# A recurrent gate and a merged feed-forward on one core: another order of all jobs, and 4 KB loads for four chunks

## The chip, the cores and the metric

The kernel runs on one core of a Trainium2 chip. A core has TensorE (PE in the profile: matrix products, into PSUM), VectorE (DVE), ScalarE (ACT), GpSimd (POOL) and SyncE (SP, which here issues the DMA transfers). The metric is the device time of one execution in microseconds.

## The reference

```python
# x, r_gate, i_gate: [4, 5824, 256]; a_param: [256]
a_base = sigmoid(a_param)
a_t    = exp(8 * sigmoid(r_gate) * log(clip(a_base, 1e-6, 1 - 1e-6)))
xg     = sqrt(max(1 - a_t * a_t, 1e-6)) * sigmoid(i_gate) * x
h      = a_t[:, t] * h + xg[:, t]          # for each t; y[:, t] = h
# y as [23296, 256]; w1, w2: [256, 1024]; w3: [1024, 1024]; w_out: [1024, 256]
out    = (((y @ w1) * (y @ w2)) @ w3) @ w_out
```

Inputs and output are f32.

## The kernel before

**Tiling.** The 23296 tokens are cut into 47 chunks: two of 256 tokens (0 and 1; their gates and their input are computed together under the name of chunk 0), 44 of 512, and one of 256 (46). Before the chunks flow, the kernel multiplies w3 by w_out once (the "fold": jobs Ft, Fc, Fm, Fe for eight pieces of w3) so that each chunk needs two products of 256 x 1024 and one of 1024 x 256.

**Jobs.** Every job has a short name, `ORDER` is a text of 2449 such words, and the last loop issues them in that order. Each engine works through its own words in that order, so the text fixes the queue of each engine. Per chunk c the words are:

- `r`, `i`, `x`: load the two gates and the input (DMA, issued by SP); `R`, `I`: tanh of a gate on ACT; `p`: plus 1 on POOL; `t c.half`: the gated input u, half a chunk at a time, on POOL (or DVE).
- `V`, `U`: turn the gate and u so that channels lie on the partitions and time runs along the row. For chunks 0, 2, 3, 4, 7 (gate) and 0, 2 to 7 (u) PE does it, for the others a transposing DMA does.
- `d c.cb`: the decay a = exp(...), on ACT, for one half cb of the channels; `s`: its square (on ACT, DVE or POOL, by the sets `AC_SQUARE` and `DV_SQUARE`); `q`: the root on ACT; `g`: the root times the turned u, on DVE (`gated`); `h c.cb`: the scan over time on DVE; `y`: the cast of h to bf16 (POOL, or by set DVE or ACT).
- `a c.mp.q`: one of the eight 128-row parts of y @ w1 on PE (two matmuls of 512 columns); `c`: its copy out of PSUM, on ACT or, for words in `DV_COPY`, on DVE; `b c.mp`: two such parts of y @ w2 on PE (four matmuls); `m c.mp`: the product of the two on DVE, into the tile `g_t`; `D c.j`: 128 rows of the last product, eight matmuls of 256 columns; `e`: copy out of PSUM (ACT, or DVE for `DV_EVAC`); `o`: store.
- `Lw`, `Cw`: load and cast of a weight; `A`: the rates from a_param; `W`: two matmuls on an identity whose result nobody reads; `E`: the identity's cast.

**Buffers.** `RINGS` gives the number of buffers of each kind: 2 for y @ w2 (`pb`), 4 PSUM banks shared by the parts of y @ w1, the last product and the turned tiles (`po`), 3 for the copies (`sa`) and for `g_t`, 2 for h, 4 for y, 6 for a and nrm. A `b` must wait until the `m` of the `b` two places earlier has read its buffer.

**Two layouts of a chunk's rows.** In most chunks, partition p holds the tokens p, p + 128, and so on, and a load reads rows of 1 KB. In the chunks for which PE turns both tiles (`long_rows`: 0, 2, 3, 4, 7), partition p holds four neighbouring tokens, a load reads 4 KB runs, and the turned tile comes out with time interleaved; `decay` and `gated` then read it with a step (`turned`) and write in order of time (`in_time`).

Of the kernel before, what the change touches and what calls it, by code (L numbers as in the profile page):

```python
# [23 lines left out]
def kernel(  # L24
# [190 lines left out]
    def decay(c, cb):  # L215
        w = width(c)
        if ("a", c) not in T:
            T["a", c] = ring(held, [P, NCB, CT], F32, name="a_t", tag="a")
# [4 lines left out]
        nc.scalar.activation(out=a, in_=pr, func=AF.Exp, scale=la4[:, cb:cb + 1], bias=la4[:, cb:cb + 1])  # L223
# [250 lines left out]
    def last(c):  # L474
# [32 lines left out]
        s7.0 I6 V5 r8 i8 V6 r9 x5 b3.3 d5.1 a3.0.1 d5.0 c3.0.1 c3.3.0 m3.3 p4 t4.0 t4.1 p5 s7.1 U4 a3.1.1 c3.1.1 s5.0  # L507
        I7 I8 D0.1 D0.0 b3.0 b3.1 a3.1.0 g4 h4.0 h4.1 s5.1 R8 R9 d6.0 d6.1 p6 y4 p8 t5.0 t5.1 D0.3 D0.2 m3.0 e0.0
        c3.1.0 a4.1.1 b4.1 a4.3.1 D2.0 D2.1 s6.1 q7 e2.0 q5 s6.0 x6 p7 t6.0 t6.1 c4.1.1 e0.1 m3.1 c4.3.1 x7 x8 o0.0
        i10 r11 V9 o2.0 a4.0.1 a4.1.0 c4.0.1 c4.1.0 m4.1 a4.2.0 b4.3 a4.3.0 U5 g5 h5.0 h5.1 c4.2.0 c4.3.0 q6 D2.3 D2.2  # L510
        e2.1 r12 r10 V8 o2.1 o0.1 i9 i11 x10 a4.0.0 U6 D3.0 a4.2.1 D3.1 b4.0 c4.0.0 I10 c4.2.1 e3.0 d9.1 d9.0 m4.3 g6
        y5 t8.1 t7.1 t7.0 m4.0 a5.1.0 b4.2 a5.1.1 a5.0.1 a5.0.0 b5.0 c5.1.1 c5.1.0 c5.0.0 m4.2 h6.1 U7 a5.3.1 c5.0.1
        s9.1 R10 c5.3.1 R11 d8.1 I9 m5.0 g7 h6.0 b5.1 D3.3 b5.3 D3.2 a5.2.1 a5.3.0 e3.1 R12 d8.0 m5.1 c5.2.1 c5.3.0
        h7.1 D4.2 a5.2.0 D4.3 e4.1 m5.3 i13 V10 o3.0 x9 p10 t8.0 y6 p9 s8.0 s9.0 h7.0 b6.0 a6.0.0 a6.0.1 y7 c5.2.0 I11
        I13 a6.2.1 a6.2.0 b5.2 s8.1 c6.0.0 c6.0.1 c6.2.0 D4.1 a6.1.0 D4.0 d10.1 c6.2.1 d10.0 e4.0 q9 a6.1.1 m6.0 m5.2
# [149 lines left out]
```

## Time and profile before

| | |
|---|---|
| time, median of 2 runs | 511.44 us (511.37 to 511.52) |
| profiled execution, first to last instruction | 509.1 us |
| PE busy | 501.7 us, 99% |
| ACT busy | 461.5 us, 91% |
| DVE busy | 431.8 us, 85% |
| POOL busy | 318.0 us, 62% |
| main DMA queue | 85.4% of 16 engines' span |

The span is that of one profiled execution, from its first to its last instruction; the time of a run has 2.3 us around it. Matmuls overlap each other in the profile: the next one starts before the modelled end of the last, so a wait shorter than this overlap does not show as idle time of PE. A row of the timeline gives start, busy time, engine, line, operation, tiles, shape and count, and in brackets the idle time in front of it and what ended it.

### The profile page before, as it was taken

How to read it: one execution, taken by the hardware profiler on the slowest of the kernel's cores; microseconds unless marked ns; L12 is line 12 of the kernel's file. 1: busy time of each engine (PE TensorE's matmuls, PEld its weight loads, DVE VectorE, ACT ScalarE, POOL GpSimd, SP SyncE). 2: the span in 40 equal slices, each digit the busy share in tenths (PEclk: the TensorE clock that was granted, in tenths of full speed). 3: DMA queues.
4: the chain of work that ended last, by engine and by line, in shares of the span. 5: the costliest groups of instructions: out<-in, count | busy, mean ns of one | idle time of the engine just before them, and what ended most of it. 6: DMA issues, size and time to landing. Idle time of an engine off the chain costs nothing.

```text
span 509.1 us, 8891 instructions
## 1 busy us (share of the span) xinstructions
PE 501.7 (99%) x3225; PEld 308.3 (61%) x3225; DVE 431.8 (85%) x417; ACT 461.5 (91%) x708; POOL 318.0 (62%) x269
## 2 busy tenths in 40 slices
...
GB/s 317 410 411 345 335 316 282 305 286 259 310 220 298 279 285 247 211 302 196 247 305 327 254 286 148 252 243 227 210 246 164 235 298 161 85 166 62 65 51 104
DMA packets 178048, 124.06 MB, mean 244 GB/s; under 512 B 87378, under 2 KB 174036, under 8 KB 178004
## 3 DMA queue, kind: packets, MB, share of 16 engines
q1 hardware_dynamic: 178000, 123.50, 85.4%
...
q14 instruction: 19, 0.16, 0.1%
...
## 4 chain that ended last, share of the span: by engine, by line
PE 92%; ACT 3%; DMA 2%; POOL 1%; DVE 1%; issue 1%; SPq 1%; ACTq 0%; DVEq 0%
PE po L357 30%; PE pb L299 29%; PE pa L299 29%; DMA wf<-in_moe_w_dram 2%; PE pw L436 1%; ACT sa L322 1%; PE ptr L200 1%; PE ptw L425 1%; POOL u_t L192 0%; DVE h_t L270 0%; SPq L151 0%; ACT ot L322 0%; SPq L407 0%; ACT L168 0%; ACT L238 0%
## 5 line engine op out<-in xcount | busy, mean ns | idle before, releaser
L337 DVE TENSOR_TENSOR g_t<-sa,pb 128x1024 bf16<-128x1024 bf16 (+1 forms) x188 | 218.7, 1180 | 58.9 <-PE pb L299 27.6
L299 PEld LDWEIGHTS <-w_sb 128*128 128x128 bf16 x1504 | 146.4, 98 | 144.1 <-issue 1.4
L322 ACT CAST sa<-pa 128x512 bf16<-128x512 f32 (+1 forms) x332 | 179.8, 591 | 27.1 <-PE pa L299 18.9
L299 PE MATMUL pa<-y_t,w_sb 128*128 128x512 bf16 (+1 forms) x752 | 190.2, 372 | 0.2 <-ACT sa L322 0.2
L299 PE MATMUL pb<-y_t,w_sb 128*128 128x512 bf16 (+1 forms) x752 | 184.9, 372 | 0.2 <-ACT w_sb L414 0.2
L357 PE MATMUL po<-wp_sb,g_t 128*128 128x256 bf16 (+1 forms) x1464 | 177.6, 272 | 0.0
L357 PEld LDWEIGHTS <-g_t 128*128 128x128 bf16 x1464 | 142.5, 98 | 39.5 <-issue 0.3
L282 POOL CAST y_t<-h_t 128x1024 bf16<-128x1024 f32 (+2 forms) x47 | 53.8, 1145 | 140.2 <-DVE h_t L270 136.1
L192 POOL TENSOR_TENSOR u_t<-i_t,x_t 128x512 bf16<-128x512 f32 (+1 forms) x90 | 123.3, 1387 | 3.8 <-DMA ut<-u_t 1.8
L270 DVE TENSOR_TENSOR_SCAN h_t<-a_t,h_t,nrm 128x512 f32<-128x512 f32 (+1 forms) x92 | 121.1, 1343 | 1.6
L233 POOL TENSOR_TENSOR nrm<-a_t 128x512 f32<-128x512 f32 x70 | 78.4, 1137 | 7.0 <-ACT a_t L223 4.0
L223 ACT ACTIVATE a_t<-rt,la 128x512 f32<-128x512 bf16 (+1 forms) x82 | 66.1, 823 | 0.0
L322 ACT COPY ot<-po 128x512 f32<-128x512 f32 x84 | 49.1, 589 | 13.2 <-PE po L357 12.9
L173 POOL TENSOR_SCALAR i_t<-i_t 128x1024 f32<-128x1024 f32 (+1 forms) x45 | 55.4, 1233 | 8.3 <-ACT i_t L168 8.3
L251 DVE SCALAR_TENSOR_TENSOR nrm<-nrm,ut 128x1024 f32<-128x1024 f32 (+1 forms) x39 | 53.2, 1365 | 5.2 <-ACT nrm L238 5.2
L168 ACT ACTIVATE i_t<-i_t 128x1024 f32<-128x1024 f32 (+1 forms) x46 | 48.5, 1063 | 0.3 <-DMA i_t<-in_i_gate_dram 0.2
L238 ACT ACTIVATE nrm<-nrm 128x1024 f32<-128x1024 f32 (+1 forms) x47 | 48.4, 1040 | 0.2
L162 ACT ACTIVATE th_r<-r_t 128x1024 bf16<-128x1024 f32 (+1 forms) x41 | 43.5, 1064 | 0.0
L320 DVE CAST sa<-pa 128x512 bf16<-128x512 f32 x36 | 23.5, 684 | 1.4 <-PE pa L299 0.8
L238 ACT ACT_TABLE_LOAD x17 | 21.8, 1283 | 0.4
L287 PE MATMUL warm<-ident 128*128 128x512 bf16 x32 | 10.7, 473 | 1.6 <-DVE ident L441 1.6
L231 ACT ACTIVATE nrm<-a_t 128x512 f32<-128x512 f32 x18 | 11.4, 645 | 0.0
...
## 6 DMA issues: line engine op xcount, KB each, us to landing
...
wf<-in_moe_w_out_dram SPq DMA_DIRECT2D x2, 512.0 KB, 10.2
rt<-th_r SPq DMA_TRANSPOSE x41, 4.7
ut<-u_t SPq DMA_TRANSPOSE x39, 4.4
```

What stands on the lines that cost most here:

```text
L173: (nc.vector if c in DV_PLUS else nc.gpsimd).tensor_scalar(t, t, 1.0, 1.0, op0=ALU.add, op1=ALU.mult)
L192: (nc.vector if (c, half) in DV_HALF else nc.gpsimd).tensor_mul(out=u, in0=t, in1=xt)
L223: nc.scalar.activation(out=a, in_=pr, func=AF.Exp, scale=la4[:, cb:cb + 1], bias=la4[:, cb:cb + 1])
L233: (nc.vector if (c, cb) in DV_SQUARE else nc.gpsimd).tensor_mul(out=n, in0=a, in1=a)
L238: nc.scalar.activation(out=n, in_=n, func=AF.Sqrt, scale=-1.0, bias=1.0)
L251: nc.vector.scalar_tensor_tensor(out=n, in0=n, scalar=1e-3, in1=T["pu", c][:, :, cols], op0=ALU.max, op1=ALU.mult)
L270: nc.vector.tensor_tensor_scan(h[:, cb, :], a[:, cb, :], n[:, cb, :], init, ALU.mult, ALU.add)
L282: (nc.vector if key in DV_CAST else nc.gpsimd).tensor_copy(out=y, in_=h)
L299: nc.tensor.matmul(out=dst, lhsT=w_sb[:, cb, m * P:(m + 1) * P], rhs=T["y", gates_of(c)][:, cb, span(c, mp)], start=(cb == 0), stop=(cb == ...
L322: nc.scalar.copy(out=dst, in_=src_ps)
L337: nc.vector.tensor_mul(out=T["g", z][:, 2 * mp:2 * mp + 2, span(c, mp)], in0=T["sa", c, mp][:, :, :w], in1=T["pb", c, mp][:, :, :w])
L357: nc.tensor.matmul(out=po, lhsT=T["g", c][:, k, j * P:(j + 1) * P], rhs=wp_sb[:, k, cols], start=(k == 0), stop=(k == KD - 1), skip_group_ ...
```

## The change

1. **A new order.** The same 2449 words in another order. The last 1049 words (from chunk 23's last product on) are the same as before, so all that moves lies in the chunks up to about 24 and in the start. With it the sets change that say which engine does a copy, a square, a copy of the result or a cast: 18 more copies go to DVE net (54 words instead of 36), 10 squares instead of 4 and 11 result copies instead of 7; two folds' copies leave DVE; two halves of u, one whole cast (chunk 24) and half of chunk 0's come to DVE; chunk 14's cast goes to ACT, and half of chunk 1's from ACT to POOL.
2. **Chunks 38 to 41** are loaded in 4 KB runs like the first ones, though a DMA turns their tiles. For 38 and 39 `decay` and `gated` read the turned bf16 tile with a step of 128 elements and write in order (`LONG_IN`); for 40 and 41 they read the bf16 tile in order and read and write the f32 tiles with a step of 4 elements (`LONG_OUT`). `gated` becomes two instructions of 512 elements per chunk instead of one of 1024.
3. **Chunk 42's scan** writes over its own input tile nrm (`OVER`) instead of into a buffer of the ring h.

```diff
--- before.py
+++ after.py
@@ -82,18 +82,20 @@
     TURN_U = {0, 2, 3, 4, 5, 6, 7}
     DV_TIMES = {0}
     DV_PLUS = set()
-    DV_HALF = set()
-    DV_SQUARE = {(0, 0), (0, 1), (5, 1), (9, 0)}
-    AC_SQUARE = {(2, 0), (2, 1), (3, 0), (4, 0), (4, 1), (5, 0), (6, 0), (6, 1), (7, 0), (8, 1), (9, 1), (11, 1), (12,
-        0), (12, 1), (13, 0), (14, 1), (15, 0), (15, 1)}
-    DV_CAST = {(1, 1)}
-    AC_CAST = {(1, 0)}
+    DV_HALF = {(5, 0), (17, 0)}
+    DV_SQUARE = {(0, 0), (0, 1), (3, 1), (13, 0), (18, 1), (19, 1), (21, 0), (23, 1), (24, 1), (28, 0)}
+    AC_SQUARE = {(2, 0), (2, 1), (3, 0), (4, 0), (4, 1), (5, 1), (7, 0), (8, 0), (8, 1), (11, 1), (12, 0), (12, 1),
+        (13, 1), (14, 1), (15, 0), (17, 1)}
+    DV_CAST = {24, (0, 1), (1, 1)}
+    AC_CAST = {14}
     DV_COPY = {(0, 0, 0), (0, 1, 0), (1, 0, 0), (1, 1, 0), (2, 0, 0), (2, 0, 1), (2, 1, 0), (2, 1, 1), (2, 2, 0), (2,
-        3, 0), (3, 0, 0), (3, 1, 0), (3, 3, 0), (4, 0, 1), (4, 1, 0), (4, 1, 1), (4, 3, 1), (5, 2, 1), (5, 3, 0), (6,
-        1, 0), (6, 1, 1), (6, 3, 1), (7, 2, 0), (8, 0, 0), (8, 0, 1), (8, 1, 0), (8, 2, 0), (9, 1, 1), (9, 2, 1), (9,
-        3, 0), (9, 3, 1), (10, 0, 0), (10, 3, 0), (11, 0, 1), (11, 1, 0), (12, 2, 0)}
-    DV_EVAC = {(0, 0), (0, 1), (4, 1), (5, 1), (6, 1), (9, 0), (9, 1)}
-    FOLD_ACT = {('e', 0), ('e', 4), ('e', 5), ('e', 7)}
+        3, 0), (3, 0, 1), (3, 1, 0), (3, 2, 0), (3, 3, 0), (4, 1, 0), (4, 1, 1), (4, 2, 1), (4, 3, 1), (5, 2, 0), (5,
+        2, 1), (6, 1, 0), (6, 1, 1), (6, 3, 1), (7, 1, 0), (7, 2, 0), (8, 0, 0), (8, 0, 1), (8, 2, 0), (8, 3, 0), (9,
+        1, 1), (9, 3, 1), (10, 0, 1), (10, 1, 1), (10, 2, 1), (11, 0, 0), (11, 0, 1), (12, 0, 1), (13, 3, 0), (14, 3,
+        0), (15, 2, 0), (16, 0, 1), (17, 2, 0), (17, 3, 0), (19, 1, 0), (20, 3, 0), (21, 3, 0), (22, 0, 0), (22, 0,
+        1), (22, 1, 0), (22, 3, 0), (23, 2, 0), (23, 2, 1), (24, 0, 1), (24, 3, 1)}
+    DV_EVAC = {(0, 0), (0, 1), (4, 0), (5, 1), (6, 1), (9, 0), (9, 1), (12, 1), (13, 0), (20, 0), (22, 1)}
+    FOLD_ACT = {('e', 0), ('e', 3), ('e', 4), ('e', 5), ('e', 6), ('e', 7)}
     FOLD_DMA = set()
     W_ACT = {('w2', 0), ('w3', 3)}
     W_DVE = {('w1', 1)}
@@ -102,6 +104,9 @@
     CASTING = set()
     WARM = [2] * 16
     HALVED = 4
+    LONG_IN = {38, 39}
+    LONG_OUT = {40, 41}
+    OVER = {42}
     RINGS = {"r": 4, "i": 5, "x": 4, "th_r": 3, "u": 2, "rt": 2, "ut": 6, "a": 6, "nrm": 6, "h": 2, "y": 4,
              "sa": 3, "g": 3, "ot": 3, "w3": 4, "w3t": 2, "po": 4, "pb": 2}
     taken = dict.fromkeys(RINGS, 0)
@@ -134,6 +139,9 @@
 
     def long_rows(c):
         return c in TURN_R and c in TURN_U
+
+    def runs(c):
+        return long_rows(c) or c in LONG_IN or c in LONG_OUT
 
     def turned(t):
         return t.rearrange("p (j q) -> p q j", q=P)
@@ -147,7 +155,7 @@
         if (nm, c) not in T:
             T[nm, c] = ring(loads, [P, 4, D], F32, name=nm + "_t", tag=nm)
         rows = src[nm][starts[c]:starts[c] + width(c), :]
-        rows = rows.rearrange("(p n) c -> p n c" if long_rows(c) else "(n p) c -> p n c", p=P)
+        rows = rows.rearrange("(p n) c -> p n c" if runs(c) else "(n p) c -> p n c", p=P)
         nc.sync.dma_start(out=T[nm, c][:, :n, cols], in_=rows[:, :, cols])
 
     def tanh_r(c, half=None):
@@ -218,8 +226,11 @@
             T["a", c] = ring(held, [P, NCB, CT], F32, name="a_t", tag="a")
         a = T["a", c][:, cb, :w]
         pr = T["pr", c, cb][:, 0, :w] if ("pr", c, cb) in T else T["pr", c][:, cb, :w]
-        if long_rows(c):
+        if long_rows(c) or c in LONG_IN:
             a, pr = in_time(a, w // P), turned(pr)
+        elif c in LONG_OUT:
+            a = in_time(a, w // P).rearrange("p q j -> p j q")
+            pr = pr.rearrange("p (j q) -> p j q", q=P)
         nc.scalar.activation(out=a, in_=pr, func=AF.Exp, scale=la4[:, cb:cb + 1], bias=la4[:, cb:cb + 1])
 
     def square(c, cb):
@@ -239,7 +250,14 @@
 
     def gated(c):
         z, cols = gates_of(c), part(c)
-        if long_rows(z):
+        if c in LONG_OUT:
+            w = width(z)
+            for cb in range(NCB):
+                n = in_time(T["n", z][:, cb, cols], w // P).rearrange("p q j -> p j q")
+                u = T["pu", z][:, cb, :w].rearrange("p (j q) -> p j q", q=P)
+                nc.vector.scalar_tensor_tensor(out=n, in0=n, scalar=1e-3, in1=u, op0=ALU.max, op1=ALU.mult)
+            return
+        if runs(z):
             w = width(z)
             j = w // P
             for cb in range(NCB):
@@ -256,7 +274,7 @@
         first = (c, "scan") not in T
         T[c, "scan"] = True
         if ("h", z) not in T:
-            T["h", z] = ring(ypool, [P, NCB, CT], F32, name="h_t", tag="h")
+            T["h", z] = T["n", z] if z in OVER else ring(ypool, [P, NCB, CT], F32, name="h_t", tag="h")
         h = T["h", z][:, :, part(c)]
         a, n = (T[key, gates_of(c)][:, :, part(c)] for key in "an")
         if first:
@@ -493,141 +511,150 @@
     }
 
     ORDER = """
-        r0 i0 x0 Lw1.1 Lw1.0 r2 i2 Lw2.0 Lw3.2 x2 E W13 A3. A0. A1. A2. R0.1 R0.0 W3 W10 V0.0 V0.1 I0 t0.1 d0.0 s0.0
-        d0.1 s0.1 q0.0 t0.0 Cw1.1 q0.1 Cw1.0 R2 I2 W5 W8 W0 U0 W4 W11 W6 W12 W7 W9 W2 g0 h0.1 h0.0 y0.1 y0.0 a0.0.1
-        a0.1.1 a0.1.0 a0.0.0 V2 W15 Cw2.0 g1 h1.1 h1.0 y1.1 y1.0 d2.1 Lw2.1 Lwo.1 Lwo.0 r3 Cw3.2 d2.0 s2.1 s2.0 q2
-        b0.0 c0.0.0 c0.1.0 a1.1.0 m0.0 Ft2 a1.1.1 c1.1.0 b0.1 a1.0.0 a0.2.1 a1.0.1 b1.1 m0.1 Fc2 b1.0 a0.2.0 p2 t2.0
-        t2.1 U2 c1.0.0 m1.1 Cw2.1 m1.0 a0.3.1 W14 b0.2 a1.3.1 W1 a1.3.0 c0.2.0 g2 Cwo.1 Cwo.0 r4 Lw3.0 Lw3.5 i3 Lw3.1
-        Lw3.4 x3 Lw3.3 Lw3.6 Lw3.7 r7 m0.2 h2.0 h2.1 R3 a1.2.1 a1.2.0 a0.3.0 c1.3.0 c0.3.0 Fm2 b0.3 b1.2 V3 R4 V4
-        c1.2.0 d3.1 d4.0 d3.0 d4.1 m0.3 b1.3 y2 Fe2 m1.2 m1.3 a2.0.0 a2.0.1 b2.0 a2.1.0 c2.0.1 c2.0.0 c2.1.0 m2.0
-        Cw3.0 s3.1 Cw3.5 Cw3.1 b2.1 a2.2.1 Ft0 a2.1.1 Fc0 Ft1 c2.1.1 Fc1 s4.0 I3 s4.1 c2.2.1 a2.2.0 Ft5 Fm0 p3 Cw3.4
-        c2.2.0 Fc5 m2.1 s3.0 q3 Cw3.3 Fe0 b2.3 Fm1 q4 Fe1 Ft4 t3.0 t3.1 U3 Fc4 g3 h3.0 h3.1 Cw3.6 Cw3.7 b2.2 Fm5 Fm4
-        a2.3.1 Ft7 R7 Fe5 Fe4 Fc7 r5 i4 r6 x4 i5 i6 i7 c2.3.1 a2.3.0 Ft3 R5 I4 c2.3.0 Fc3 Ft6 Fm7 y3 a3.2.1 Fc6 Fm3
-        m2.3 R6 Fe7 c3.2.1 V7 m2.2 Fe3 d7.1 a3.2.0 c3.2.0 d7.0 b3.2 Fm6 a3.3.1 a3.0.0 a3.3.0 m3.2 Fe6 c3.0.0 I5 c3.3.1
...
+        r0 E W7 W1 A3. A0. i0 W8 A1. A2. R0.1 W14 R0.0 I0 V0.1 V0.0 x0 t0.0 W0 Lw1.1 W5 d0.0 s0.0 t0.1 U0 d0.1
+        s0.1 W13 W2 W15 Lw1.0 Cw1.1 q0.0 r2 W4 i2 g0 Lw2.0 q0.1 Lw3.2 g1 W9 W10 W6 W12 R2 x2 W11 h0.1 h0.0 Cw1.0
+        I2 y0.1 y0.0 a0.1.0 a0.1.1 a0.0.0 a0.0.1 Lw2.1 Lwo.0 h1.1 h1.0 c0.1.0 Lwo.1 p2 y1.1 r3 V2 c0.0.0 Cw2.0
+        d2.1 r4 d2.0 s2.1 Lw3.5 b0.1 m0.1 b0.0 m0.0 y1.0 a1.1.0 a1.1.1 Cw3.2 Lw3.1 s2.0 t2.0 q2 Lw3.0 t2.1
+        c1.1.0 a1.0.0 a1.3.0 a1.0.1 c1.0.0 Ft2 a0.2.1 Fc2 Cw2.1 Lw3.4 b1.1 m1.1 b1.0 a0.2.0 i3 c0.2.0 U2 m1.0
+        a1.3.1 c1.3.0 Lw3.6 g2 Cwo.0 b0.2 a0.3.1 m0.2 a0.3.0 R3 a1.2.1 Cwo.1 a1.2.0 Fm2 h2.0 W3 c0.3.0 h2.1 b0.3
+        m0.3 R4 Fe2 c1.2.0 b1.2 m1.2 V3 d3.0 x3 V4 b1.3 d3.1 y2 a2.0.1 m1.3 Cw3.1 c2.0.1 Lw3.7 a2.0.0 c2.0.0
+        Lw3.3 b2.0 a2.1.0 c2.1.0 d4.1 d4.0 a2.1.1 c2.1.1 Cw3.0 Ft0 Fc0 s4.1 s3.1 r7 Ft1 s4.0 s3.0 I3 a2.2.0
+        a2.2.1 c2.2.1 Fc1 c2.2.0 m2.0 b2.1 m2.1 r6 Cw3.5 q3 Fm0 Cw3.4 Ft4 Ft5 Fe0 Fm1 q4 R7 Fc4 b2.3 p3 t3.0
+        t3.1 Cw3.3 U3 b2.2 Fe1 Fc5 Fm5 g3 Fe5 h3.0 h3.1 Fm4 Fe4 a2.3.1 c2.3.1 Cw3.6 Cw3.7 Ft7 a2.3.0 Fc7 y3 r5
+        Ft3 R5 i4 I4 Ft6 c2.3.0 Fm7 Fe7 a3.2.1 c3.2.1 Fc3 p4 Fm3 Fc6 R6 V7 i6 m2.3 x4 t4.0 Fe3 d7.0 m2.2 i5 I5
...
```

The lines of the order that are left out differ likewise up to the common end.

More of the change, by code (lines that the diff above doesn't have):

```diff
@@ L506 @@
-        m2.3 R6 Fe7 c3.2.1 V7 m2.2 Fe3 d7.1 a3.2.0 c3.2.0 d7.0 b3.2 Fm6 a3.3.1 a3.0.0 a3.3.0 m3.2 Fe6 c3.0.0 I5 c3.3.1
[L507 to L515, printed above, removed]
@@ new lines @@
+        c6.1.0 R12 p11 d10.0 o3.1 q9 D4.0 e4.0 p10 x11 a6.1.1 b6.1 c6.1.1 a6.3.1 s10.1 m6.1 r14 b6.2 m6.2 a7.3.0
+        s8.1 a6.3.0 c6.3.0 a7.1.0 c7.3.0 q8 c6.3.1 b6.3 c7.1.0 m6.3 a7.3.1 I12 t9.1 p13 x10 t10.1 r15 g8 c7.3.1
+        t10.0 V11 U9 g9 d11.1 a7.0.1 c7.0.1 o4.0 h8.0 a7.1.1 h8.1 h9.1 c7.1.1 b7.1 m7.1 o4.1 x12 D6.1 D6.0 e6.0
+        i16 I16 r16 b7.3 d11.0 V12 U10 s11.1 d12.1 m7.3 a7.0.0 D5.0 c7.0.0 D5.1 e5.0 d12.0 D6.2 p16 a7.2.1
+        c7.2.1 D6.3 e6.1 b7.0 m7.0 x13 y8 a8.2.1 a8.2.0 s10.0 c8.2.0 a7.2.0 c7.2.0 a8.0.1 c8.0.1 c8.2.1 t11.1
@@ new lines @@
+        t17.1 U17 e12.1 m13.3 o11.1 a15.1.1 s19.1 c15.1.1 a15.0.1 b14.2 m14.2 c15.0.1 a15.1.0 c15.1.0 R23
+        a14.3.0 s20.1 s18.1 c14.3.0 p18 b15.0 m15.0 V21 d21.0 a14.3.1 b15.1 t18.1 c14.3.1 a15.2.1 c15.2.1 h16.1
+        a15.2.0 D13.3 d21.1 c15.2.0 D13.1 x21 D13.0 e13.0 m15.1 s17.1 q17 x19 y16 b14.3 q18 a16.0.0 m14.3 D13.2
+        e13.1 c16.0.0 t19.0 b15.2 m15.2 t18.0 U18 x20 i22 a16.1.0 c16.1.0 q19 o12.1 a16.1.1 g17 x22 s20.0 t19.1
+        U19 V22 c16.1.1 a15.3.0 c15.3.0 a16.0.1 c16.0.1 b16.0 q20 m16.0 a16.2.0 h17.0 h17.1 c16.2.0 b15.3 t20.0
```

238 lines of the change are left out of this document (123 added, 115 removed).

## The prediction, made before the changed kernel ran

> **What bounds the kernel now.** I read the page of the profile first, then the engines in stretches, then the start on the timeline, since the page names one engine so clearly.
>
> ```profile
> span 509.1 us, 8891 instructions
> PE 501.7 (99%) x3225; PEld 308.3 (61%) x3225; DVE 431.8 (85%) x417; ACT 461.5 (91%) x708; POOL 318.0 (62%) x269
> ...
> PE 92%; ACT 3%; DMA 2%; POOL 1%; DVE 1%; issue 1%; SPq 1%; ACTq 0%; DVEq 0%
> ...
> 20.00:140.00 120.00, 119.91 (x838) 76.59 (x839) 117.88 (x133) 116.87 (x169) 84.59 (x71) 1.00 1.07 321
> 140.00:285.00 145.00, 145.00 (x890) 86.92 (x889) 126.08 (x104) 141.79 (x219) 103.65 (x84) 1.00 0.96 265
> 285.00:400.00 115.00, 114.82 (x706) 68.78 (x705) 95.00 (x77) 108.87 (x170) 78.81 (x64) 1.00 0.87 223
> 400.00:445.00 45.00, 45.00 (x285) 27.64 (x283) 38.05 (x32) 39.56 (x65) 27.76 (x22) 1.00 0.67 196
> ```
>
> The first three lines are the page's: PE is busy 501.7 of 509.1 us, and 92% of the chain that ended last is PE. The four stretches (length, then busy us and count of PE, weight load, DVE, ACT, POOL, then PE's clock, the DMA share and GB/s) say where the other 7.4 us lie. Between 20 and 445 us PE lacks 0.09 + 0.18 = 0.27 us, at a granted clock of 1.00. So the rest is at the two ends. The change leaves PE's instructions alone: the words are the same, and the two sets that say what PE turns are not touched. What can be won is therefore idle time of PE plus the `W` matmuls (their result is not read) that stand between real ones. That is a matter of the first 23 us:
>
> ```profile
> 7.08 0.69 DVE L189 SCALAR_TENSOR_TENSOR u_t<-i_t,x_t 128x512 bf16<-128x512 f32 x1 [1.62 <-DMA x_t<-in_x_dram]
> ...
> 7.69 1.29 DVE L233 TENSOR_TENSOR nrm<-a_t 128x512 f32<-128x512 f32 x2
> ...
> 8.89 0.69 DVE L189 SCALAR_TENSOR_TENSOR u_t<-i_t,x_t 128x512 bf16<-128x512 f32 x1
> ...
> 9.31 1.15 ACT L238 ACTIVATE nrm<-nrm 128x512 f32<-128x512 f32 x2
> ...
> 9.63 0.62 PE L200 MATMUL ptr<-ident,u_t 128*128 128x128 bf16 x8 [0.54 <-DVE u_t L189]
> ...
> 10.09 3.19 PE L287 MATMUL warm<-ident 128*128 128x512 bf16 x14
> ...
> 10.36 0.75 DVE L248 SCALAR_TENSOR_TENSOR nrm<-nrm,ptr 128x256 f32<-128x256 f32 x2 [0.18 <-PE ptr L200]
> ...
> 11.14 1.37 DVE L270 TENSOR_TENSOR_SCAN h_t<-a_t,nrm 128x256 f32<-128x256 f32 x2
> ...
> 11.99 1.06 POOL L282 CAST y_t<-h_t 128x256 bf16<-128x256 f32 x2 [0.61 <-DVE h_t L270]
> ...
> 13.11 1.04 PE L299 MATMUL pa<-y_t,w_sb 128*128 128x256 bf16 x8
> ...
> 14.43 0.59 PE L287 MATMUL warm<-ident 128*128 128x512 bf16 x2
> ...
> 15.22 0.61 PE L299 MATMUL pb<-y_t,w_sb 128*128 128x256 bf16 x4 [0.19 <-ACT w_sb L414]
> ...
> 15.67 0.38 PE L299 MATMUL pa<-y_t,w_sb 128*128 128x256 bf16 x2
> ...
> 16.47 0.62 PE L425 MATMUL ptw<-ident,w_t 128*128 128x128 bf16 x8 [0.43 <-POOL w_t L416]
> ...
> 17.52 2.50 POOL L192 TENSOR_TENSOR u_t<-i_t,x_t 128x512 bf16<-128x512 f32 x2
> ...
> 19.34 0.28 PE L200 MATMUL ptr<-ident,u_t 128*128 128x128 bf16 x2
> ...
> 20.07 0.51 PE L200 MATMUL ptr<-ident,u_t 128*128 128x128 bf16 x6 [0.46 <-POOL u_t L192]
> ...
> 20.64 0.59 PE L287 MATMUL warm<-ident 128*128 128x512 bf16 x2
> ...
> 20.95 2.02 POOL L416 CAST wo_sb<-wf 128x1024 bf16<-128x1024 f32 x2
> ...
> 21.08 0.60 PE L299 MATMUL pb<-y_t,w_sb 128*128 128x256 bf16 x4
> ...
> 21.73 0.59 PE L287 MATMUL warm<-ident 128*128 128x512 bf16 x2
> ```
>
> The real work starts at 13.11, when chunk 0's cast is done. From there I count what PE loses, from start to start, since the busy times overlap. Two warm matmuls take 21.08 - 20.64 = 0.44 us, so one takes 0.22; two matmuls of 256 columns take half of that, 0.22. At 14.43: 15.22 - 14.43 = 0.79 (a `W`, then a wait for w2's cast). At 15.67: 16.47 - 15.67 - 0.22 = 0.58 (w3's cast on POOL). At 19.34: 20.07 - 19.34, less two transposes of 128 columns, 0.055 each by the same rate, leaves 0.62 (u of chunk 2, which POOL made from 17.52 to 20.02). The `W` at 20.64 and at 21.73: 0.44 each. Sum 2.87 us. Waits below 0.16 us (a matmul's modelled overlap) can hide later; I set them to nothing.
>
> **The change part by part.**
>
> *The start, until the first real matmul.* SP issues the same ten loads first in the same order. On DVE the order after x arrives becomes u, square, u, square instead of u, square, square, u. By the rows above that is four instructions of about 0.60 us each from 7.08, so the second square ends at 9.57 instead of 8.98. The root, which began at 9.31, begins at about 9.6, and PE turns u at about 9.1 instead of 9.63. Both meet at `g0`, which so starts near 10.3, as now (10.36). Then `g1` is put ahead of chunk 0's two scans: another 0.72 us (0.75 by the row, less the overlap). Against it half of chunk 0's cast goes to DVE, and POOL has one cast (0.55) where it had two (1.06). Sum: the first real matmul at about 13.5 to 13.6, **0.45 us later**. Nine `W` words, or 18 x 0.22 = 4.0 us, now lie between the turned u and that point; from 9.6 that is 13.6, so they just fit, and are free.
>
> *The start, after it.* Only one `W` is left among real work (0.44 us), against three. The five parts `a` that now stand ahead of the first fold cover the wait for w3's cast, which POOL makes at about 15.5 to 16.5; `p2` is ahead of it on POOL, so u of chunk 2 is done near 19.05 (16.55 + 2.50) instead of 20.02, and PE gets there near 19. The waits of 0.58 and 0.62 go, and of the 0.79 the wait part, about 0.35, goes or is taken by the later start. What is late next is w_out: its two casts come behind w2's second on POOL, end near 22.1 (19.05 + 1.0 + 2.02), and the fold's first product stands about 0.7 us earlier in PE's queue. I charge **0.7 us** for that wait. Queued behind it on PE are chunk 0's and 1's last parts, and DVE's products of these wait with them. So the start: -2.87 + 0.44 + 0.45 + 0.7 = **-1.3 us**.
>
> *Chunks 2 to 12 (until 140 us).* DVE is at 117.88 of 120, and this is where more work on it would hurt. Counting the words of the sets up to chunk 12: one copy more, one square fewer, one result copy more, one half of u more, two small fold copies fewer.
>
> ```profile
> L320 DVE CAST sa<-pa 128x512 bf16<-128x512 f32 x36 | 23.5, 684 | 1.4 <-PE pa L299 0.8
> ...
> L233 DVE TENSOR_TENSOR nrm<-a_t 128x512 f32<-128x512 f32 x4 | 2.6, 682 | 0.0
> ...
> L223 ACT ACTIVATE a_t<-rt,la 128x512 f32<-128x512 bf16 x80 | 65.0, 828 | 0.0
> ...
> L223 ACT ACTIVATE a_t<-ptr,la 128x512 f32<-128x512 bf16 x10 | 7.2, 773 | 0.2 <-PE ptr L200 0.2
> ...
> L248 DVE SCALAR_TENSOR_TENSOR nrm<-nrm,ptr 128x512 f32<-128x512 f32 x8 | 5.1, 681 | 0.0
> ...
> L251 DVE SCALAR_TENSOR_TENSOR nrm<-nrm,ut 128x1024 f32<-128x1024 f32 x38 | 52.5, 1382 | 5.2 <-ACT nrm L238 5.2
> ...
> 428.71 1.03 POOL L282 CAST y_t<-h_t 128x1024 bf16<-128x1024 f32 x1
> ...
> 431.15 1.03 PE L299 MATMUL pa<-y_t,w_sb 128*128 128x512 bf16 x4
> ```
>
> (Groups with shapes kept apart: count, busy us, mean ns, idle; the last two rows are the timeline's.) A copy or a square holds DVE 0.60 us when the next one follows (7.69 to 8.89 for two). Net about 0.60 + 0.60 - 0.7 = +0.5 us on DVE's 2.12 us of idle time. Nothing on PE.
>
> *Chunks 13 to 24 (140 to 285 us).* Here lie 17 of the 18 net copies, seven squares (one of them, chunk 28's, later), three result copies, a half of u and a cast: 17 + 7 + 3 + 1 + 1 = 29 instructions, 29 x 0.60 = 17.4 us on DVE, which is idle 145.00 - 126.08 = 18.9 us there. Its 104 instructions also overlap by up to 0.08 us each when they follow without a gap, some 8 us. So about 9 us stay. ACT, at 141.79 of 145, gets lighter by the same instructions. I take nothing for PE. If the cover is gone, that is if the additions come bunched, it is DVE's products that are late, and PE waits in its next `b`.
>
> *Chunks 38 to 41.* Twelve loads in runs of 4 KB: the DMA share there is 0.67, and no row of PE waits for a load; nothing. The stepped accesses: eight decays on ACT and eight halves of `gated` on DVE. The rows nearest to them are the first chunks', which read PSUM with the same step: 773 ns against 828, and 2 x 681 against 1382. So the step costs nothing there, and I take nothing. No row shows a step in SBUF, nor a stepped write. From below, a gain of 8 x 0.05 us on ACT, as in those rows; from above I take three times the duration: per chunk `gated` then costs 2 x 2 x 0.681 = 2.7 us more. Chunk 40's cast ends at 429.74 and PE starts on it at 431.15, so 1.4 us are covered. The Trainium skill, page "SBUF — State Buffer", section "Door 1", says that accesses which go to a new 16-byte line each time pay a penalty, and names no price for DVE or ACT; the steps of 256 and 16 bytes here do that. The PSUM rows speak against a large price, though that page gives PSUM even shorter lines; no row shows SBUF.
>
> *Chunk 42's scan in place.* Same instruction; chunks 43 to 45 take the other h buffer. PE has no idle time up to 445 us that a buffer of h could end. Nothing.
>
> **Sum.** 509.1 - 1.3 = 507.8 us for the profiled execution; with the 2.3 us around it (511.44 - 509.1) **510.2 us**.
>
> **The rivals.**
>
> *The start gives nothing back.* The gains there are waits for weights and POOL; if these come no earlier (the DMA share is 1.07 until 140 us), the later first matmul and w_out's wait remain and the waits of 0.58 and 0.62 return: -1.3 + 1.2 + a few tenths of new waits, 511.3 to 512.5 us. For it: the casts follow the loads. Against it: two waits were for POOL, whose order changes.
>
> *DVE becomes the bound in chunks 13 to 24: slower.* If its instructions keep their full 0.68 us and the added ones don't fall into its idle time, 29 x 0.68 = 19.7 us meet 18.9, and bunching makes PE wait some 0.3 us in each of 12 chunks: 510.2 + 0.8 + 3.6 = 514.6 us. It decides once DVE's idle time in 140 to 285 us is below 2 us. Against it: until 140 us DVE has just 2.1 us of idle time, and PE lost 0.09.
>
> *Stepped accesses cost three times.* 4 x 2.7 = 10.9 us on DVE against 45.00 - 38.05 = 6.95 idle in 400 to 445: 4.0 us late, 514.2 us. By the rule of the Trainium skill named above this would be the place. For it: no row of SBUF. Against: the PSUM rows.
>
> *The start is all won.* Without the later start and w_out's wait: -2.87 + 0.44, and up to 0.3 of hidden waits: 508.7 us.
>
> **How the numbers follow.** The forecast (509.2 to 511.3) has a chance of 0.55, the start that gives nothing back 0.20, DVE as the bound 0.11, the steps 0.04, all won 0.10. The range from 508.3 to 513.5 takes in the first, the second and the last, and the lesser part of the slower ones; about 0.12 is left out. A measurement here tells about 2%, or 10.2 us, from no change. Faster than 501.2 us would need more than the idle time and the three warm words: 0.01. Slower than 521.7 needs PE to wait 10 us, more than each slower rival gives: 0.04. Within: 0.95.
>
> **What would show it.** The first `pa` matmul near 13.5 us; no idle time of PE at the first fold and at chunk 2's turned u; a wait near 21.5 us at line 436. DVE at about 95% in 140 to 285 us and PE still at 145 of 145. The new `decay` and `gated` rows near 0.8 and 0.68 us. Wrong if PE shows waits on DVE's `g_t` in chunks 13 to 24, or if `gated` rows above 1.4 us stand at 400 to 440 us.

## The result, and the profile after

The changed kernel takes 537.85 us (median of 2 runs, 536.92 to 538.77) against 511.44: ratio 1.0516 (95% interval 1.0494 to 1.0538). It is 5% slower; the forecast was 510.2. The page of the changed kernel:

```profile
span 537.0 us, 8857 instructions
...
PE 505.2 (94%) x3169; PEld 308.4 (57%) x3225; DVE 453.3 (84%) x451; ACT 458.4 (85%) x686; POOL 304.8 (57%) x261
...
PE 39%; ACT 22%; DMA 18%; issue 7%; DVE 7%; SPq 5%; POOL 1%; ACTq 0%; DVEq 0%; POOLq 0%
```

PE does the same work, in a span 27.9 us longer, and its share of the chain that ended last falls from 92% to 39%. ACT, the transfers and SP's queue take its place. (This trace lacks 56 matmul records, x3169 for x3225 weight loads, so PE's busy times below are low by up to 0.2 us for each record missed.) The same stretches as in the prediction:

```profile
20.00:140.00 120.00, 110.04 (x749) 69.30 (x763) 110.05 (x121) 108.18 (x152) 76.33 (x68) 1.00 1.05 305
140.00:285.00 145.00, 137.78 (x830) 82.32 (x845) 133.84 (x127) 126.80 (x189) 82.07 (x67) 1.00 0.87 230
285.00:400.00 115.00, 111.19 (x661) 65.54 (x673) 93.38 (x79) 107.42 (x163) 79.23 (x63) 1.00 0.97 253
400.00:445.00 45.00, 41.85 (x256) 25.46 (x258) 37.98 (x33) 36.97 (x57) 26.65 (x22) 0.98 0.76 211
```

PE, which lacked 0.27 us between 20 and 445 us, now lacks 10.0, 7.2, 3.8 and 3.2. ACT falls from 116.87 to 108.18 and from 141.79 to 126.80. Some of the second fall is work that the new sets give to DVE, which rises from 126.08 to 133.84 there; but ACT also stands still. What it waits for is in the table of waits. Before:

```profile
POOL u_t L192 <- DMA ut<-u_t: 1.8, 2, 1.1
...
ACT th_r L160 <- DMA r_t<-in_r_gate_dram: 0.8, 1, 0.8
...
ACT i_t L168 <- DMA i_t<-in_i_gate_dram: 0.2, 1, 0.2
```

After (engine, line and what was waited for; us in total, times, longest):

```profile
ACT a_t L234 <- DMA rt<-th_r: 8.2, 5, 2.8
ACT i_t L176 <- DMA i_t<-in_i_gate_dram: 6.8, 6, 2.8
ACT ot L340 <- DMA out_dram<-ot: 3.5, 5, 1.1
ACT th_r L170 <- DMA r_t<-in_r_gate_dram: 1.7, 2, 1.1
...
POOL u_t L200 <- DMA x_t<-in_x_dram: 11.1, 8, 3.8
...
POOL u_t L200 <- DMA ut<-u_t: 5.2, 3, 2.2
```

That is 36.5 us of waiting for transfers on ACT and POOL, against 2.8 us in the rows of before. How one of these waits reaches PE is seen on the timelines of SP, ACT and PE near 100 us:

```profile
93.45 0.52 SPq L159 DMA_DIRECT2D i_t<-in_i_gate_dram  x1
```

```profile
96.32 0.61 ACT L340 COPY ot<-po 128x512 f32<-128x512 f32 x1
99.77 1.06 ACT L176 ACTIVATE i_t<-i_t 128x1024 f32<-128x1024 f32 x1 [2.84 <-DMA i_t<-in_i_gate_dram]
100.73 0.80 ACT L234 ACTIVATE a_t<-rt,la 128x512 f32<-128x512 bf16 x1
101.44 0.61 ACT L242 ACTIVATE nrm<-a_t 128x512 f32<-128x512 f32 x1
102.17 0.81 ACT L234 ACTIVATE a_t<-rt,la 128x512 f32<-128x512 bf16 x1
102.89 0.56 ACT L340 CAST sa<-pa 128x512 bf16<-128x512 f32 x1
```

```profile
100.12 1.03 PE L317 MATMUL pb<-y_t,w_sb 128*128 128x512 bf16 x4
103.51 1.51 PE L317 MATMUL pa<-y_t,w_sb 128*128 128x512 bf16 x6 [2.36 <-ACT sa L340]
```

SP issues the load of a gate i from 93.45 to 93.97; in the new order its word, `i16`, stands directly ahead of its reader, `I16`. ACT comes to its tanh at 96.93 and stands still until 99.77, with three short jobs queued behind the tanh and then the copy `sa` that PE needs. That copy ends at 103.45 and PE starts at 103.51, 2.36 us late. PE's own table of waits names ACT's copies and DVE's `g_t`, never a load, which is how the cause hides. Its largest rows:

```profile
PE pb L317 <- DVE g_t L355: 6.9, 8, 2.2
PE pa L317 <- ACT sa L340: 6.1, 7, 2.4
PE pa L317 <- ACT ot L340: 5.8, 7, 1.4
```

### The profile page after: what moved, and what is told of

Read it like the earlier page. It is cut to its first block, busy times and chain, and to the rows that moved or that the text cites. A ratio compares the mean times of both kernels' runs of the same rounds, so it can differ in the third digit from the quotient of the medians.

```text
span 537.0 us, 8857 instructions
## 1 busy us (share of the span) xinstructions
PE 505.2 (94%) x3169; PEld 308.4 (57%) x3225; DVE 453.3 (84%) x451; ACT 458.4 (85%) x686; POOL 304.8 (57%) x261
## 4 chain that ended last, share of the span: by engine, by line
PE 39%; ACT 22%; DMA 18%; issue 7%; DVE 7%; SPq 5%; POOL 1%; ACTq 0%; DVEq 0%; POOLq 0%
PE pa L317 13%; PE pb L317 13%; PE po L375 12%; ACT sa L340 8%; DMA r_t<-in_r_gate_dram 4%; ACT a_t L234 4%; DMA out_dram<-ot 4%; DMA rt<-th_r 3%; SPq L219 3%; DVE g_t L355 3%; DMA i_t<-in_i_gate_dram 3%; ACT th_r L170 3%; ACT ot L340 2%; DVE h_t L288 2%; DMA wf<-in_moe_w_dram 2%
## 5 line engine op out<-in xcount | busy, mean ns | idle before, releaser
L340 ACT CAST sa<-pa 128x512 bf16<-128x512 f32 (+1 forms) x314 | 170.5, 590 | 38.8 <-PE pa L317 28.1
L317 PE MATMUL pb<-y_t,w_sb 128*128 128x512 bf16 (+1 forms) x730 | 182.1, 372 | 8.5 <-DVE g_t L355 6.9
L300 POOL CAST y_t<-h_t 128x1024 bf16<-128x1024 f32 (+2 forms) x44 | 45.8, 1041 | 146.4 <-DVE h_t L288 138.6
L288 DVE TENSOR_TENSOR_SCAN h_t<-a_t,h_t,nrm 128x512 f32<-128x512 f32 (+1 forms) x88 | 112.7, 1311 | 1.1
L244 POOL TENSOR_TENSOR nrm<-a_t 128x512 f32<-128x512 f32 x66 | 75.0, 1149 | 15.0 <-ACT a_t L234 11.1
L234 ACT ACTIVATE a_t<-rt,la 128x512 f32<-128x512 bf16 (+1 forms) x82 | 70.1, 867 | 8.3 <-DMA rt<-th_r 8.2
L340 ACT COPY ot<-po 128x512 f32<-128x512 f32 x80 | 46.7, 587 | 15.5 <-PE po L375 11.1
L269 DVE SCALAR_TENSOR_TENSOR nrm<-nrm,ut 128x1024 f32<-128x1024 f32 (+1 forms) x35 | 49.2, 1405 | 4.9 <-ACT nrm L249 2.5
L338 DVE CAST sa<-pa 128x512 bf16<-128x512 f32 x54 | 35.7, 682 | 2.4 <-remote 1.3
L338 DVE COPY ot<-po 128x512 f32<-128x512 f32 (+2 forms) x13 | 8.1, 633 | 6.8 <-PE po L375 6.5
```

The lines of the kernel that those rows point to most:

```text
L244: (nc.vector if (c, cb) in DV_SQUARE else nc.gpsimd).tensor_mul(out=n, in0=a, in1=a)
L269: nc.vector.scalar_tensor_tensor(out=n, in0=n, scalar=1e-3, in1=T["pu", c][:, :, cols], op0=ALU.max, op1=ALU.mult)
L288: nc.vector.tensor_tensor_scan(h[:, cb, :], a[:, cb, :], n[:, cb, :], init, ALU.mult, ALU.add)
L317: nc.tensor.matmul(out=dst, lhsT=w_sb[:, cb, m * P:(m + 1) * P], rhs=T["y", gates_of(c)][:, cb, span(c, mp)], start=(cb == 0), stop=(cb == ...
L340: nc.scalar.copy(out=dst, in_=src_ps)
```

## The experiments

The theories at the outset: the new order brings loads too late; the new order or sets overload DVE or ACT; the stepped accesses cost more than the PSUM rows said. Times are medians; the kernel before had medians of 511.0 to 511.7 beside them.

**e1: the order alone** (sets included, nothing on chunks 38 to 42).

```diff
-    LONG_IN = {38, 39}
-    LONG_OUT = {40, 41}
-    OVER = {42}
+    LONG_IN = set()
+    LONG_OUT = set()
+    OVER = set()
```

> The changed kernel without the 4 KB loads, the stepped accesses and the scan in place; its order and its sets stay. Theory 'order': the new queues of the engines cost the time (in the profile after, ACT waits 16.7 us for transfers and PE waits for ACT's and DVE's copies all along from 20 to 300 us), so 529 to 534 us: what goes is at most the loss between 400 and 445 us. Theory 'steps': the stepped accesses of chunks 38 to 41, which took 1.06 to 1.3 us instead of 0.68 on DVE, cost most of it: 512 to 516 us.

532.54 us, ratio 1.0416 (1.0375 to 1.0458). **e2: the other half alone**, the three sets above in the kernel before with its own order:

> The kernel before with the 4 KB loads of chunks 38 to 41, their stepped accesses and chunk 42's scan in place alone. Theory 'order': 512 to 516 us, the stepped accesses being some 8 x 0.4 + 8 x 0.5 us longer on engines with idle time. Theory 'steps': 528 us or more.

516.05 us, 1.0095 (1.0076 to 1.0115). So the order with its sets costs some 21 us, the edits of chunks 38 to 42 some 5 us, and the parts add up. From 310 to 480 us, where e1 has the words of before again, its PE is busy 168.37 of 170 us (169.82 before): the loss lies where the words moved.

**e3: the loads put back** to where the kernel before has them, all else of the changed kernel kept.

```diff
- ... m7.1 o4.1 x12 D6.1 D6.0 ...
+ ... e5.1 r14 x12 x13 t13.0 ...
```

> The changed kernel with the loads r, i, x alone taken out of its order and put back in the order of before, each at the same amount of TensorE work as there; all other words keep the new order. Theory 'late loads': the new order issues loads later against their use (half of them have 6 us of TensorE work between load and tanh instead of 9), ACT waits for them and its copies queue behind: 515 to 523 us. Theory 'order without the loads' (stores, transposes and compute queues): 532 us or more.

568.51 us, 1.1127 (1.1087 to 1.1167): much worse than the changed kernel, where the theory of late loads put it at 515 to 523 (the excerpt shows x12 alone, 60 words later). Places that serve one order don't serve another.

**e4: the new order with the sets of before**, and **e7: the order of before with the new sets.**

```diff
-    DV_SQUARE = {(0, 0), (0, 1), (3, 1), (13, 0), ...
+    DV_SQUARE = {(0, 0), (0, 1), (5, 1), (9, 0)}
...
```

> The changed kernel with the sets of before: the copies, squares, casts and evacuations go to the engines of before, the order of the words stays the new one. Theory 'engines': the 29 instructions that DVE gets in chunks 13 to 24 make it the bound: 512 to 520 us without them. Theory 'late loads': ACT gets 18 copies back and the waits stay: 535 to 545 us.

561.72 us, 1.0988 (1.0957 to 1.1018): above both ranges.

> The kernel before with the new sets (18 more copies, 6 more squares and 4 more evacuations on DVE) in the old order. If DVE's 18 us more are what costs time: 525 us or more. If an engine's load matters little and sets and order only have to fit each other: 512 to 522 us.

535.54 us, 1.0472 (1.0451 to 1.0492). The new order is worse with the old sets than with the new ones (561.72 against 537.85). The new sets cost 24 us in the old order, where the theory of DVE's additional work put them, and about what they cost together with the new order (532.54 in e1; the two intervals meet). So sets and order have to be judged together. e7 also has its own kind of loss: ACT and POOL wait only 1.1 and 1.3 us for transfers, DVE has 15% of its chain, and among PE's waits stands one for a copy on DVE:

```profile
PE 62%; DVE 15%; DMA 8%; ACT 6%; issue 5%; POOL 3%; SPq 0%; DVEq 0%; ACTq 0%; POOLq 0%
```

```profile
PE po L359 <- DVE sa L322: 4.9, 1, 4.9
```

**e5: all loads ahead** by up to 5 us of PE's work, and **e6: the stores back** by 5 us, so that SP is not held by a store; both from e1.

```diff
- ... D3.1 e3.0 x8 i10 I10 r12 y5 ...
+ ... q6 D2.3 x8 i10 r12 e2.1 ...
```

(e5; the three loads x8, i10 and r12 stand 18 or 19 words earlier.)

> The new order alone (as in the second run of this study's first kernel: no 4 KB loads, no scan in place), 532.5 us, with each load r, i, x moved ahead by up to 5 us of TensorE work as far as its buffer allows; so the loads pass stores and transposes in SP's queue, and nothing else moves. Theory 'late loads': ACT's and POOL's waits for i and x (17 us) go, 515 to 524 us. Theory 'compute queues' (the order on ACT, DVE and PE itself): 529 to 536 us.

562.32 us, 1.097 (1.0882 to 1.1058), above both ranges. ACT's waits for gates are down to 0.4 us and POOL's for x to 4.1 from 10.3; those for the transposing transfers and stores that now stand behind the loads have grown:

```profile
ACT a_t L234 <- DMA rt<-th_r: 26.9, 7, 7.5
...
ACT ot L340 <- DMA out_dram<-ot: 20.8, 7, 6.1
...
POOL u_t L200 <- DMA ut<-u_t: 17.4, 5, 8.0
```

```diff
- ... d18.1 h16.0 o12.0 s19.0 b13.2 ...
+ ... a15.0.1 b14.2 o12.0 m14.2 ...
```

> The new order alone, 532.5 us, with each store moved back by 5 us of TensorE work as far as its buffer allows, so that a store that waits for its copy on ACT holds up fewer loads and transposes behind it on SP. Theory 'SP is held by stores' (SP waits 123 us for copies, 100 us before): 518 to 527 us. Theory 'compute queues': 530 to 540 us, the upper end since three buffers of ot then come free later.

550.82 us, 1.0754 (1.0711 to 1.0796), above both ranges. SP waits less for the copies that its stores need (52.6 us for ACT's `ot` against 116.8 in e1), but ACT then waits 22.8 us for stores to free `ot`, against 3.9. What the holding of SP by stores costs by itself, this run can't say.

**e8: the kernel before with its loads 5 us back.** Nothing of the change is in it.

```diff
- ... D2.2 e2.1 r12 r10 V8 o2.1 ...
+ ... b4.2 r12 r10 i9 i11 x10 a5.1.1 ...
```

> The kernel before with each load r, i, x moved back by 5 us of TensorE work (never behind its use). Theory 'late loads': this alone makes it 520 to 535 us. Theory 'compute queues': 511 to 515 us.

549.95 us, 1.0751 (1.0721 to 1.0782). The old order too loses 38 us when its loads stand 5 us later, more than the theory of late loads gave.

**e9: e1 without the loads** of chunks 8 to 46.

```diff
+        if c >= 8:
+            T[nm, c] = T["x" if nm == "i" else nm, 4]
+            return
...
```

> The kernel of the order alone (532.5 us), with the loads of the gates and inputs of chunks 8 to 46 left out: these chunks read chunk 4's tiles, so their gates and inputs are chunk 4's. All other words stay in the new order. If the new order loses its 21 us because ACT and POOL wait for loads and for the transposing transfers behind them, the time falls to 512 to 516 us. If the order of the compute queues loses them by itself, it stays at 528 or above. In between, both take part, in that share.

512.38 us, 1.002 (1.001 to 1.0029). This decides most. The same order, sets and compute queues, and PE is full again (the same two first stretches):

```profile
20.00:140.00 120.00, 117.95 (x809) 75.08 (x822) 117.10 (x132) 115.97 (x166) 80.92 (x72) 1.00 0.57 170
140.00:285.00 145.00, 143.90 (x874) 86.72 (x889) 139.47 (x132) 133.38 (x198) 90.56 (x72) 1.00 0.43 108
```

DVE is busier here (139.47) than in the changed kernel (133.84), and PE is not late for it. What e9 leaves out are the loads' places and their DMA work together: the DMA share falls to 0.57 and 0.43.

**e10 and e11: lighter ACT, lighter DVE**, both from e1.

```diff
-        n = T["n", c][:, :, cols]
+        n = T["n", c][:, :, cols] if c < 8 else T["n", c][:, 0, cols]
         nc.scalar.activation(out=n, in_=n, func=AF.Sqrt, scale=-1.0, bias=1.0)
```

> The kernel of the order alone (532.5 us), with the roots of chunks 8 to 46 taken over one half of the channels only, which leaves out half of that step and makes each such root on ACT about 0.48 us shorter, some 18 us in all. If the order loses time where PE waits for a full ACT queue, at least half of the 21 us comes back: 522 us or less. If ACT's waits for transfers are the cause, ACT is only earlier at the same transfer: 529 us or above.

533.16 us, 1.0429 (1.0406 to 1.0453).

```diff
-        n = T["n", c][:, :, cols]
+        ch = slice(None) if c < 8 else 0
+        n = T["n", c][:, ch, cols]
...
```

> The kernel of the order alone (532.5 us), with the gated input of chunks 8 to 46 made for one half of the channels only, which leaves out half of that step and makes each such instruction on DVE about 0.65 us shorter, some 25 us in all. If the order loses time because DVE's additional copies and squares come bunched ahead of the products that PE waits for, at least half of the 21 us comes back: 522 us or less. If DVE only passes on the lateness of ACT or of transfers: 528 us or above.

533.56 us, 1.0431 (1.04 to 1.0463). ACT is busy 440.3 us in e10, DVE 431.4 in e11, 14 and 20 us less than in e1, and nothing comes back. Neither engine's load by itself is the cause, and ACT's waits for i and for turned gates stay: 7.1 and 8.0 us in e10, 4.6 and 9.8 in e11, 7.0 and 6.6 in e1.

**e13: e1 with half of the loads' bytes.**

```diff
+        m = 1 if 8 <= c < 46 and nm != "i" else n
-        nc.sync.dma_start(out=T[nm, c][:, :n, cols], in_=rows[:, :, cols])
+        nc.sync.dma_start(out=T[nm, c][:, :m, cols], in_=rows[:, :m, cols])
...
```

> The kernel of the order alone (532.5 us). Of r and x of chunks 8 to 45 each load moves one quarter of its rows, and the other three quarters of the tile are computed from that one, so those gates and inputs are not the reference's. Every load stays with its place, its buffer and its waits; the loads' bytes of these chunks fall by half. If the new order loses its time because transfers queue behind each other on busy DMA engines, the time falls to 512 to 516 us. If the loads hold SP at their places whatever their size, 526 us or above.

517.43 us, 1.0119 (1.0095 to 1.0144): 15 of the 21 us are back, with every load at its place. The loads of i keep their length here, and ACT's waits for them fall all the same, from 7.0 to 1.4 us: they land sooner (median 4.7 us after issue for 5.2), and so do the transposing transfers of the gates (3.0 for 4.6). **e16: the same cut in e8:**

> The kernel before with its loads 5 us of PE's work further back, which gave 549.95 us, and with the loads of r and x of chunks 8 to 45 cut to one quarter of their rows as above. If late places cost because the transfers are long, most of the 38 us goes: 512 to 520 us. If the places by themselves cost it, 540 us or above.

539.78 us, 1.0554 (1.0513 to 1.0595): 10 of 38 us, a result between the two expectations and nearer to the second. ACT's waits for i, which was not cut, stay (18.1 us for 19.2 in e8); those of ACT and POOL for r and x, which were, fall from 30.8 to 19.7. So loads moved 5 us back are late even when they are short, though less. **e14: the kernel before, with more packets.**

```diff
-        nc.sync.dma_start(out=T[nm, c][:, :n, cols], in_=rows[:, :, cols])
+        for cols in (cols,) if c < 8 else (slice(0, P), slice(P, D)):
+            nc.sync.dma_start(out=T[nm, c][:, :n, cols], in_=rows[:, :, cols])
```

> The kernel before, in its own order and with its own sets, with every load of chunks 8 to 46 made as two transfers of 512-byte runs (the two halves of the channels) in place of one with 1 KB runs. Same bytes, same places. If the DMA engines have no room until 300 us, where their share is 0.9 to 1.09, the additional packets cost 20 us or more, so 530 us or above. If only places and waits in SP's queue count, 511 to 516 us.

512.99 us, 1.0032 (1.0021 to 1.0044). Its DMA share is higher than the changed kernel's:

```profile
20.00:140.00 120.00, 118.07 (x815) 75.59 (x830) 117.20 (x132) 115.39 (x167) 82.44 (x70) 1.00 1.12 315
140.00:285.00 145.00, 144.09 (x875) 86.93 (x890) 124.93 (x104) 141.24 (x218) 101.22 (x83) 1.00 1.03 263
```

1.12 and 1.03 against 1.05 and 0.87. A DMA system as busy as that costs 1.7 us where the places suit, so a high share does not by itself cost time. In the new order less DMA work helps (e13), as it would where loads have no time to spare; a load's own length and what else the queue moves are not told apart by these runs.

**e17 and e18: only the latest loads.** I counted PE's work (0.216 us for a matmul of 512 columns, from start to start, and in proportion) between a load's word and the first word that reads it. In chunks 8 to 28 of the new order 17 loads have less than 4 us, in the order before 8, while a load takes 5 to 6 us from issue to landing (median, in both). It is a rough sign only: SP runs ahead at times (it issued `i16` 3.5 us before ACT came to `I16`), and the 8 cost the order before hardly a wait. e18 leaves the 17 out; e17 moves them ahead.

```diff
+        if (nm, c) in LATE:
+            return
...
```

> The kernel of the order alone (532.5 us), with these 17 of the 117 loads of chunks 8 to 46 left out; their chunks compute with the tile of an earlier chunk (or, for a gate i, with one of r), so those values are not the reference's. If these late loads carry the loss, most of the 21 us comes back: 512 to 519 us. If the loss is spread over all loads, 17 of 117 bring back about 3 us: 528 to 531 us.

524.12 us, 1.0262 (1.0213 to 1.0312): 8 of 21 us, between the two expectations; more than twice their share in number, and not most of the loss.

> The kernel of the order alone (532.5 us), with the 17 loads of chunks 8 to 28 that stand less than 4 us of PE's work ahead of their first reader moved ahead to some 7.5 us (i16 to 3.5, for its buffer comes free no sooner); no other word is moved among the rest. If these late loads are the cause and SP reaches the new places in time, 512 to 522 us. If loads put ahead only push the transposing transfers and stores behind them, as when all loads were moved, 535 us or above.

535.4 us, 1.0466 (1.0437 to 1.0495): no gain. The waits for i fall from 7.0 us in e1 to 0.6, POOL's for x stay (10.0 for 10.3), those for turned gates rise from 6.6 to 16.3:

```profile
ACT a_t L234 <- DMA rt<-th_r: 16.3, 7, 4.9
...
ACT i_t L176 <- DMA i_t<-in_i_gate_dram: 0.6, 1, 0.6
```

**e12 and e15: the stepped chunks apart**, in the kernel before.

```diff
     LONG_IN = set()
     LONG_OUT = {40, 41}
     OVER = set()
```

> The kernel before, with chunks 40 and 41 alone loaded in 4 KB runs and their f32 tiles written with a step of 4 elements; nothing for 38, 39 and 42. All three edits together gave 516.05 us, 4.8 us over the kernel before. If the stepped accesses are what costs, and alike in reading and writing, 513 to 514.5 us; if the scan in place (1.66 to 1.8 us by its rows there, against 1.3) or the stepped reads cost the most, 512.5 us or less.

514.59 us, 1.0065 (1.005 to 1.008). With `LONG_IN = {38, 39}` alone:

> The kernel before, with chunks 38 and 39 alone loaded in 4 KB runs and their turned tiles read with a step of 128 elements. All three edits gave 516.05 us, the stepped writes of 40 and 41 alone 514.6 us. If each stepped chunk costs alike, 513 to 514.5 us; if the stepped writes are the dear ones, or chunks 38 and 39 have room that 40 and 41 lack, 511.5 to 512.5 us.

512.35 us, 1.0017 (1.0008 to 1.0026). The stepped writes cost 3.2 us, the stepped reads 1.1. Of e2's 5.0 us that leaves less than a microsecond, no more than the intervals, for the scan in place, which was not run alone. In the kernel with stepped writes (e12) PE's longest wait after the start shows the path:

```profile
414.92 2.93 DVE L256 SCALAR_TENSOR_TENSOR nrm<-nrm,ut 128x512 f32<-128x512 f32 x2
...
417.70 2.33 DVE L353 TENSOR_TENSOR g_t<-sa,pb 128x1024 bf16<-128x1024 bf16 x2
...
418.95 1.02 PE L315 MATMUL pb<-y_t,w_sb 128*128 128x512 bf16 x4 [1.60 <-DVE g_t L353]
```

The two halves of `gated` hold DVE 2.93 us, the product `g_t` stands behind them, and the next `b` waits for it.

## Why the prediction was wrong

**The bound.** Right that PE was full and that little could be won. Wrong was what I made of it: that PE stays full unless the change shows it a new wait.

**The start: near in size, by luck.** The forecast was -1.3 us.

```profile
13.11 1.03 PE L317 MATMUL pa<-y_t,w_sb 128*128 128x256 bf16 x8
13.98 0.61 PE L208 MATMUL ptr<-ident,th_r 128*128 128x128 bf16 x8
15.03 1.05 PE L317 MATMUL pb<-y_t,w_sb 128*128 128x256 bf16 x8 [0.43 <-ACT w_sb L432]
...
17.00 0.61 PE L443 MATMUL ptw<-ident,w_t 128*128 128x128 bf16 x8
17.66 0.38 PE L317 MATMUL pa<-y_t,w_sb 128*128 128x256 bf16 x2
...
19.46 0.38 PE L317 MATMUL pa<-y_t,w_sb 128*128 128x256 bf16 x2
20.09 0.61 PE L317 MATMUL pb<-y_t,w_sb 128*128 128x256 bf16 x4 [0.25 <-POOL w_sb L434]
20.74 1.03 PE L317 MATMUL pa<-y_t,w_sb 128*128 128x256 bf16 x8
21.61 1.04 PE L454 MATMUL pw<-wo_sb,w3t 128*128 128x256 bf16 x8
22.49 0.59 PE L305 MATMUL warm<-ident 128*128 128x512 bf16 x2
```

Counted as there: 15.03 - 13.98 - 0.44 = 0.61, 17.66 - 17.00 - 0.44 = 0.22, 20.09 - 19.46 - 0.22 = 0.41, 20.74 - 20.09 - 0.43 = 0.22 and one pair of `W`, 0.43; together 1.89 against 2.87, a gain of 1.0 us. The make-up differs from mine: the first real matmul is no later (13.11 both times; I charged 0.45), the wait for w_out that I charged at 0.7 is not there, and instead waits of 1.46 us remain, those for w2's casts among them, where I had counted on almost none. The two errors nearly cancel. After 24 us the gain is lost.

**Chunks 2 to 24: the step that failed.** "Nothing on PE" and "I take nothing for PE" were worth 21 us (e1, order and sets). I counted instructions against each engine's idle time in long stretches; by that count the order fits, and e9 shows that the count itself was fair: without the loads it runs at 512.4 us. What I left out are the transfers. "No row of PE waits for a load" was written of chunks 38 to 41, and I took it for the whole kernel; PE has no such row after the change either. Waits for transfers show on ACT and POOL, at the head of their queues, and on PE only as a late copy. The prediction quoted a DMA share of 1.07 and 0.96 and made a rival of it in the start only. What was missing is a count of how long ahead of its reader each moved load stands, against the 5 to 6 us that it takes.

What the runs show of the mechanism: the loss passes through the loads (e9), not through the work of ACT or of DVE alone (e10, e11); a busier DMA system by itself costs the old order little (e14); fewer bytes undo most of the loss (e13), and the 17 latest loads carry more than their share (e18). Three ways of moving loads alone did not cure it (e3, e5, e17): in e5 and e17 the waits went over to transposing transfers and stores, which SP issues from the same queue. That these share a loop, in which a late ACT makes SP's next issues late and those make ACT later, is my reading of the timelines and was not tested by itself. Open is also how the loss divides between the places of the loads and what stands ahead of each in the queue, and what part the sets have: they cost 24 us in the old order with hardly a wait for a transfer (e7), and with the new order next to nothing once the loads are gone (e9).

**Chunks 38 to 41: mis-sized.** I took nothing, by the PSUM rows. The groups of the changed kernel, shapes apart (count, busy us, mean ns):

```profile
L269 DVE SCALAR_TENSOR_TENSOR nrm<-nrm,ut 128x1024 f32<-128x1024 f32 x34 | 48.5, 1426 | 4.9 <-ACT nrm L249 2.5 <-DMA ut<-u_t 2.3
...
L266 DVE SCALAR_TENSOR_TENSOR nrm<-nrm,ptr 128x512 f32<-128x512 f32 x8 | 5.1, 679 | 0.3 <-PE ptr L208 0.3
L258 DVE SCALAR_TENSOR_TENSOR nrm<-nrm,ut 128x512 f32<-128x512 f32 x4 | 5.0, 1296 | 1.2 <-ACT nrm L249 1.2
...
L266 DVE SCALAR_TENSOR_TENSOR nrm<-nrm,ut 128x512 f32<-128x512 f32 x4 | 4.1, 1064 | 0.0
...
L288 DVE TENSOR_TENSOR_SCAN nrm<-a_t,h_t,nrm 128x512 f32<-128x512 f32 x2 | 3.5, 1805 | 0.0
```

The same 512 elements with the same step take 679 ns from PSUM and 1064 ns from SBUF; with a stepped f32 tile in SBUF the mean is 1296. That mean hides one long row (shortest, median and longest, in ns):

```profile
L258 DVE SCALAR_TENSOR_TENSOR nrm<-nrm,ut x4: 1089/1100/1897, 438.1 to 462.7; 128x512 f32<-128x512 f32 x4
```

Three of the four take 1.09 to 1.11 us, as much as the other step. Unstepped rows of `gated` are long at times as well (median 1.25 us for 1024 elements, longest 2.19), so the long one is not put down to the step. The decays of these chunks take 1.3 us for 0.82. The cost is about 1.6 times, between my value and my upper bound. The mechanism and the place of the rival "stepped accesses" were right, its price of three times was not. The rule of the Trainium skill, page "SBUF — State Buffer", section "Door 1", that accesses which go to a new 16-byte line each time pay, agrees with these rows of SBUF; I let the PSUM rows outweigh it, and they were rows of another memory.

**The scan in place: open.** I wrote "Same instruction". The group above has 1805 ns where the scans into h have 1336, but it is two instructions, of 1.62 and 1.99 us, and scans into h take up to 2.23 us too. No run shows that the place costs.

**DVE as the bound in chunks 13 to 24**, my slower rival, was not what happened: DVE's busy time in 140 to 285 us is 133.84 of 145, PE waits there only 0.5 us for `g_t`, and e11 gained nothing from a lighter DVE.
